# Two constants of a kernel's own scheduler: the transfer of loads planned a fifth longer, and six PSUM banks for attention in place of seven

## The chip, the cores and the metric

The kernel runs on one core of a Trainium2 chip. The metric is device time in microseconds (us), the median of several executions. One execution of each kernel was also profiled. Its span, from the first to the last instruction, is shorter than its own time (384.8 against 386.56 us for the kernel before). Comparisons between traces therefore use trace times alone.

Names: PE is TensorE (matmul), PEld its weight loads, DVE is VectorE, ACT is ScalarE, POOL is GpSimd, and SP is SyncE, which only issues DMAs here. A name such as SPq or POOLq is an engine's instruction queue. The argument rests on engines that keep to the order in which the program holds their instructions.

## The reference

A linear attention with a feature map comes first, then a feed-forward network (FFN) with a squared ReLU. There are 8 batches, 8 heads, 576 positions and a head dimension of 64.

```python
def phi(x):                                   # (b, h, s, 64) -> (b, h, s, 256)
    proj = einsum('bhsd,df->bhsf', x, w_phi)
    proj = proj - max(abs(proj), axis=-1, keepdims=True)
    return concatenate([exp(proj), exp(-proj)], axis=-1)
q_p, k_p = phi(q), phi(k)
kv, z = einsum('bhsf,bhsd->bhfd', k_p, v), sum(k_p, axis=2)
attn = einsum('bhsf,bhfd->bhsd', q_p, kv) / (einsum('bhsf,bhf->bhs', q_p, z)[..., None] + 1e-06)
x = attn.transpose(0, 2, 1, 3).reshape(4608, 512)
h = maximum(x @ w_in, 0.0)                    # w_in: 512 x 2048
out = (h * h) @ w_out                         # w_out: 2048 x 512
```

The FFN works on nine *chunks* of four tiles of 128 tokens. Each batch of attention makes four and a half such tiles. Below, a unit or a chunk starts when its first weight load does.

## The kernel before

The kernel does not write its instructions down in the order of its source. It first describes every piece of work as an `Op`, with an engine, a planned cost, a key for priority, the ops it depends on, and the buffers it takes. Then `Plan.order()` plays this list through in planned time, and the program is emitted in the order of the planned starts. The constants of the plan thus decide the order in which instructions stand in each engine's queue, and with it which buffer each op takes and how much filler PE gets. When the program runs, an instruction waits for its data and for the instruction ahead of it in its queue. The planned times exist no more.

```python
NATT, LEAD, DUE, SPAN = 7, 3, 26, 36
r_one = ring("one", 8, [P, 512], F32, ps)     # the eight PSUM banks
r_att = Ring(list(range(NATT)))               # so many of them may attention hold at once
...
def load(key, kb, rows, fn, deps=(), bufs=()):
    ...
    i = pl.op("pool", 780, key, fn, list(deps) + (full if n > 4096 else []), bufs, lat=0)
    issues.append(i)
    d = pl.op("dma", kb * 2.5, key, None, [i], bufs, lat=2600)   # planned transfer
    queue.append((n, d))
    return d
```

Four parts:

```python
# POOL issues the three loads (k, q, v) of a batch
nc.gpsimd.dma_start(out=buf.t[...], in_=rows[:, a:z, :])                 # L301

# SP transposes a finished attention tile into the FFN's input by a DMA
nc.sync.dma_start_transpose(out=xT.t[:, tt], in_=xo.t)                   # L652

# FFN in: one unit is four 512-column matmuls on PE; all units read the chunk's xT
nc.tensor.matmul(out=w.t[...], lhsT=win[...], rhs=xT.t[:, a:z, kc, :])   # L675
# then ACT applies ReLU (L680), and POOL squares, for chunks 0 to 6
nc.gpsimd.tensor_tensor(out=t.t, in0=r.t, in1=r.t, op=ALU.mult)          # L683
```

The DMA transposes of q and k (L352) are issued by SP as well. While PE has nothing to do at the start, the plan fills it with matmuls on a tile of ones (`warm`, L322), which are meant to keep its clock up.

Of the kernel before, what the change touches and what calls it, by code (L numbers as in the profile page):

```python
# [45 lines left out]
class Plan:  # L46
# [31 lines left out]
    def order(self):  # L78
        ready = {e: [] for e in sorted({o.eng for o in self.ops}, key=lambda e: (e != "x", e))}
        busy = {e: 0.0 for e in ready}  # L80
        rows = {e: None for e in ready}
        for o in self.ops:
            if o.n == 0:
                heapq.heappush(ready[o.eng], (o.key, o.seq, o))
        ev, now, done = [], 0.0, []

        def can(o):
            new = [x for x in o.bufs if x.slot is None]
            return all(x.can() and len(x.ring.free) >= sum(y.ring is x.ring for y in new)
                       for x in new)  # L90

        while True:
            for e, q in ready.items():
                if busy[e] > now:
                    continue
                skip = []
                while q:
                    it = heapq.heappop(q)
                    o = it[2]
                    if not can(o):  # L100
                        skip.append(it)
                        continue
                    for x in o.bufs:
                        if x.slot is None:
                            x.take()
                    o.start = now
                    end = now + o.cost
                    if o.rows is not None:
                        if rows[e] not in (None, o.rows):
                            end += self.SWITCH  # L110
                        rows[e] = o.rows
                    busy[e] = end
                    done.append(o)
                    same = [d for d in o.next if d.eng == e]
                    other = [d for d in o.next if d.eng != e]
                    for i, (t, what) in enumerate((
                            (end, ()), (end + 60, same), (end + o.lat, other),
                            (end + o.lat, None))):
                        heapq.heappush(ev, (t, 4 * o.seq + i, o, what))
                    break  # L120
                for it in skip:
                    heapq.heappush(q, it)
                if busy[e] <= now and e in self.idle and self.idle[e][2].start is None:
                    cost, fn, _ = self.idle[e]
                    o = Op()
                    o.eng, o.fn, o.start, o.cost, o.key = e, fn, now, cost(now), 1e9
                    busy[e] = now + o.cost
                    done.append(o)
                    heapq.heappush(ev, (busy[e], -len(done), o, ()))
            if not ev:  # L130
                break
            now = ev[0][0]
            while ev and ev[0][0] <= now:
                _, _, o, what = heapq.heappop(ev)
                if what is None:
                    for x in o.bufs:
                        x.left -= 1
                        if x.left == 0:
                            x.ring.free.append(x.slot)
                    continue  # L140
                for d in what:
                    d.n -= 1
                    if d.n == 0:
                        heapq.heappush(ready[d.eng], (d.key, d.seq, d))
        assert all(o.start is not None for o in self.ops)
        self.span = now
        return done
# [10 lines left out]
def kernel(  # L158
# [58 lines left out]
    r_h2 = ring("h2", 30, [P, TCH], BF16)  # L217
    r_ot = ring("ot", 2, [P, DM], F32)

    NATT, LEAD, DUE, SPAN = 7, 3, 26, 36  # L220

    r_one = ring("one", 8, [P, 512], F32, ps)
    r_att = Ring(list(range(NATT)))
# [2 lines left out]
    pl = Plan()  # L226
# [27 lines left out]
    def load(key, kb, rows, fn, deps=(), bufs=()):  # L254



        n = (queue[-1][0] if queue else 0) + rows
        full = [d for m, d in queue if m >= n - 4096][:1]
        i = pl.op("pool", 780, key, fn, list(deps) + (full if n > 4096 else []), bufs, lat=0)  # L260
        issues.append(i)
        d = pl.op("dma", kb * 2.5, key, None, [i], bufs, lat=2600)
        queue.append((n, d))
        return d

# [27 lines left out]
    def loads(b, dep=None):  # L293
        got = {}
        for i, (name, src, r) in enumerate((("k", k, r_xk), ("q", q, r_xq), ("v", v, r_xv))):
            buf = Buf(r)
            rows = src[b].rearrange("h s d -> (h s d)").rearrange(
                "(pr t c) -> t pr c", pr=NPR, t=P)

            def fn(a, z, buf=buf, rows=rows):  # L300
                nc.gpsimd.dma_start(  # L301
                    out=buf.t[:, a * NJ : z * NJ].rearrange("t (pr j) d -> t pr (j d)", j=NJ),
                    in_=rows[:, a:z, :],
                )
            key = FIRST + i if b == 0 else FIRST + (10, 13, 14)[i] if b == 1 else 32 * b - 120
            cut = (0, 2, 4) if b == 0 else (0, 4)
            got[name] = buf, [[load(key, 295 * (z - a), 128 * (z - a),
                                    lambda a=a, z=z, fn=fn: fn(a, z), [dep], [buf])]
                              for a, z in zip(cut, cut[1:])]
        return got  # L310
# [3 lines left out]
    win_v = moe_w_in.rearrange("(kc p) m -> p kc m", p=P)  # L314
    wout_v = moe_w_out.rearrange("(kc p) n -> p kc n", p=P)
    o_win = load(FIRST + 5, 4194, 512, lambda: nc.gpsimd.dma_start(out=win, in_=win_v))
    x1 = loads(1)
    o_wout = load(FIRST + 12, 4194, 2048, lambda: nc.gpsimd.dma_start(out=wout, in_=wout_v))

    def warm():  # L320
# [486 lines left out]
```

## Time and profile before

| | before |
|---|---|
| time | 386.79 us, median of 3 (385.71 to 387.05) |
| span of the profiled run | 384.8 us |
| PE busy | 368.5 us, 96% |
| filler matmuls | 274 |
| PE idle in the trace, gaps over 0.35 us, with the 1.1 us before its first matmul | 10.3 us |

The page of the kernel before, its head and three of its rows over 40 slices of 9.6 us each. A digit is tenths of a slice; PEclk is the clock that PE was granted.

```profile
span 384.8 us, 10484 instructions
...
PE 368.5 (96%) x4152; PEld 199.6 (52%) x4152; DVE 248.0 (64%) x554; ACT 244.1 (63%) x485; POOL 184.7 (48%) x310
...
PE   8899799999994999999999999999999999999994
...
PEclk9999989999996999999999999999999999999999
DMA  8999994349989442389559563964311232112123
```

PE is full in nearly every slice. The Trainium skill ("Trainium Kernel Development and Optimization", "Performance Expectations") warns that matmul busy time says little about the distance from the roofline, since matmuls are pipelined. It is used here only to find the holes, and a hole is where it is low. The table by windows (columns: window, its length, then busy us and instructions of PE, PEld, DVE, ACT, POOL, then granted clock, DMA share, GB/s; the DMA share adds up the times of packets, and these overlap, so it can pass 1) shows the two holes of the kernel before.

```profile
44.00:50.00 6.00, 3.94 (x50) 3.04 (x50) 5.72 (x11) 5.71 (x8) 5.15 (x5) 0.97 1.27 164
50.00:54.00 4.00, 4.00 (x76) 2.40 (x75) 3.83 (x11) 1.55 (x4) 1.25 (x2) 0.61 1.22 201
...
115.60:121.00 5.40, 0.57 (x5) 0.25 (x4) 3.23 (x7) 2.00 (x2) 0.00 (x0) 0.72 1.15 185
121.00:125.00 4.00, 4.00 (x14) 1.26 (x15) 0.42 (x1) 1.42 (x3) 0.37 (x2) 0.53 1.19 242
```

In the second hole PE does almost nothing for 5.4 us. It then works for 4 us at about half the clock. The chain of waits (start, length, what) names the cause.

```profile
109.27 1.26 SPq L352
110.53 0.04 issue
110.57 10.29 DMA qT_76<-xq_71
120.87 0.05 issue
120.91 0.28 PE one_157 L561
121.19 1.82 PE one_160 L704 x4
```

PE stood at the query projection of batch 3 (L561). Its input is a DMA transpose that took 10.29 us from issue to landing. The timeline of POOL shows what was under way then: the three loads of batch 4, issued from 108.72 us on.

```profile
108.72 0.81 POOL L301 DMA_DIRECT2D xk_68<-in_k_dram  x1 [0.36 <-issue]
109.52 0.75 POOL L301 DMA_DIRECT2D xq_70<-in_q_dram  x1
110.25 0.76 POOL L301 DMA_DIRECT2D xv_72<-in_v_dram  x1
```

### The profile page before, as it was taken

How to read it: one execution, taken by the hardware profiler on the slowest of the kernel's cores; microseconds unless marked ns; L12 is line 12 of the kernel's file. 1: busy time of each engine (PE TensorE's matmuls, PEld its weight loads, DVE VectorE, ACT ScalarE, POOL GpSimd, SP SyncE). 2: the span in 40 equal slices, each digit the busy share in tenths (PEclk: the TensorE clock that was granted, in tenths of full speed). 3: DMA queues.
4: the chain of work that ended last, by engine and by line, in shares of the span. 5: the costliest groups of instructions: out<-in, count | busy, mean ns of one | idle time of the engine just before them, and what ended most of it. 6: DMA issues, size and time to landing. Idle time of an engine off the chain costs nothing.

```text
span 384.8 us, 10484 instructions
## 1 busy us (share of the span) xinstructions
PE 368.5 (96%) x4152; PEld 199.6 (52%) x4152; DVE 248.0 (64%) x554; ACT 244.1 (63%) x485; POOL 184.7 (48%) x310
## 2 busy tenths in 40 slices
PE   8899799999994999999999999999999999999994
PEld 7788656544551455545544544455445454444442
DVE  2878977994693747894798468947893764233221
ACT  4795879568943796588649775887588653333300
POOL 8543846439940696297556656575445320000000
PEclk9999989999996999999999999999999999999999
DMA  8999994349989442389559563964311232112123
GB/s 124 211 208 204 168 188 87 75 75 210 101 126 206 89 57 48 72 139 151 111 89 200 80 115 63 200 121 95 70 27 31 49 64 53 44 27 55 28 61 75
DMA packets 70720, 40.39 MB, mean 105 GB/s; under 512 B 51088, under 2 KB 65552, under 8 KB 70672
## 3 DMA queue, kind: packets, MB, share of 16 engines
q1 hardware_dynamic: 55360, 21.38, 31.3%
q0 software_dynamic: 15312, 18.35, 29.1%
q8 instruction: 32, 0.52, 0.6%
q14 instruction: 16, 0.13, 0.1%
HBM read 36.77 MB, written 9.44 MB: 120 GB/s over the span
## 4 chain that ended last, share of the span: by engine, by line
PE 84%; DVE 7%; DMA 3%; ACT 2%; POOL 1%; SPq 1%; issue 1%; DVEq 0%
PE one_163 L704 6%; PE one_164 L675 5%; PE one_161 L704 5%; PE one_159 L704 5%; PE one_162 L675 4%; PE one_157 L675 4%; PE one_159 L675 4%; PE one_163 L675 4%; PE one_157 L704 4%; PE one_162 L704 4%; PE one_160 L675 3%; PE one_161 L675 3%; PE one_160 L704 3%; PE one_164 L322 3%; PE one_158 L675 3%; DMA qT_76<-xq_71 3%
## 5 line engine op out<-in xcount | busy, mean ns | idle before, releaser
L675 PEld LDWEIGHTS <-win 128*128 128x128 bf16 x704 | 59.2, 98 | 55.6 <-issue 5.2
L322 PE MATMUL one_164<-ones 128*128 128x128 bf16 x274 | 20.8, 233 | 1.1 <-DVE scrap L280 1.1
L574 POOL COPY mq_107<-m_104 64x4 f32<-64x4 f32 x52 | 9.6, 184 | 20.9 <-DVE m_104 L565 16.6
L322 PEld LDWEIGHTS <-ones 128*128 128x128 bf16 x274 | 17.6, 105 | 2.4 <-DVE scrap L280 1.1
L574 POOL COPY mq_108<-m_105 64x4 f32<-64x4 f32 x46 | 8.5, 184 | 11.7 <-DVE m_105 L565 10.3
L406 PEld LDWEIGHTS <-kT_74 64*128 64x128 bf16 x288 | 8.2, 94 | 8.8 <-issue 7.2
L574 POOL COPY mq_109<-m_106 64x4 f32<-64x4 f32 x46 | 8.5, 184 | 8.3 <-DVE m_106 L565 6.8
L680 ACT ACTIVATE hr_124<-one_160 128x512 bf16<-128x512 f32 x9 | 5.4, 596 | 8.6 <-PE one_160 L675 8.1
L683 POOL TENSOR_TENSOR h_141<-hr_123 128x512 bf16<-128x512 bf16 x4 | 4.2, 1039 | 11.6 <-ACT hr_123 L680 10.2
L675 PE MATMUL one_163<-xT_118,win 128*128 128x128 bf16 (+2 forms) x88 | 9.4, 253 | 0.3 <-ACT em_111 L581 0.2
L680 ACT ACTIVATE hr_123<-one_163 128x512 bf16<-128x512 f32 x9 | 5.3, 592 | 6.3 <-PE one_163 L675 5.7
L680 ACT ACTIVATE hr_122<-one_162 128x512 bf16<-128x512 f32 x9 | 5.4, 597 | 5.4 <-PE one_162 L675 5.3
L565 DVE TENSOR_REDUCE m_104<-one_162 128x4 f32<-128x512 f32 x6 | 4.1, 688 | 7.0 <-ACT hr_122 L680 4.9
L461 POOL TENSOR_TENSOR va_90<-xv_72,va_90 128x512 bf16<-128x512 bf16 (+1 forms) x5 | 6.2, 1244 | 5.0 <-ACT kph_80 L448 4.4
L561 PEld LDWEIGHTS <-qT_76 64*128 64x128 bf16 x144 | 4.4, 94 | 7.5 <-DMA qT_76<-xq_71 5.2
L683 POOL TENSOR_TENSOR h_143<-hr_122 128x512 bf16<-128x512 bf16 x4 | 4.2, 1044 | 8.3 <-ACT hr_122 L680 8.3
L532 PEld LDWEIGHTS <-wphi_61 64*128 64x128 bf16 x160 | 4.8, 94 | 6.2 <-issue 5.0
L435 ACT ACTIVATE kph_79<-ksh_88 128x1024 bf16<-128x1024 f32 x5 | 5.3, 1055 | 4.3 <-DVE ksh_88 L427 4.2
L610 PEld LDWEIGHTS <-qph_97 128*128 128x128 bf16 (+1 forms) x104 | 5.4, 101 | 4.7 <-issue 1.7
L680 ACT ACTIVATE hr_123<-one_161 128x512 bf16<-128x512 f32 x8 | 4.8, 604 | 4.3 <-PE one_161 L675 3.6
L565 DVE TENSOR_REDUCE m_105<-one_164 128x4 f32<-128x512 f32 (+1 forms) x7 | 4.5, 646 | 4.6 <-PE one_161 L561 4.1
L680 ACT ACTIVATE hr_123<-one_164 128x512 bf16<-128x512 f32 x9 | 5.4, 596 | 3.1 <-PE one_164 L675 3.1
(1001 smaller groups left out, 1365.2 us busy)
## 6 DMA issues: line engine op xcount, KB each, us to landing
out_dram<-ot_155 SPq DMA_DIRECT2D x36, 128.0 KB, 2.4
out_dram<-ot_156 SPq DMA_DIRECT2D x36, 128.0 KB, 2.4
xk_69<-in_k_dram POOLq DMA_DIRECT2D x4, 576.0 KB, 6.8
xq_71<-in_q_dram POOLq DMA_DIRECT2D x4, 576.0 KB, 9.9
xv_73<-in_v_dram POOLq DMA_DIRECT2D x4, 576.0 KB, 12.9
win<-in_moe_w_in_dram POOLq DMA_DIRECT2D x1, 2048.0 KB, 18.4
wout<-in_moe_w_out_dram POOLq DMA_DIRECT2D x1, 2048.0 KB, 31.0
xk_68<-in_k_dram POOLq DMA_DIRECT2D x3, 576.0 KB, 7.4
```

The lines of the kernel that those rows point to most:

```text
L322: nc.tensor.matmul(out=r_one.tiles[7][:, :P], lhsT=ones, rhs=ones, start=True, stop=True)
L406: nc.tensor.matmul(out=w[e].t[:, i * Fd : (i + 1) * Fd], lhsT=kT.t[r, u0 // 2 + i, :], rhs=wphi2[r, :], start=True, stop=True)
L435: nc.scalar.activation(out=t.t[:, :, : n // 2, :].rearrange("x e i f -> x e (i f)"), in_=ksh.t[:, :, : n // 2, :].rearrange("x e i f -> x ...
L461: v_.tensor_tensor(out=y.t[:, u0 : u0 + n, :D], in0=xv.t[:, u0 : u0 + n, :], in1=y.t[:, u0 : u0 + n, D].to_broadcast([P, n, D]), op=ALU.mult)
L532: nc.tensor.matmul(out=o[bk][:, r], lhsT=wphi2[x, :], rhs=qT.t[x, m : m + nj, :].rearrange("x m (hi p) -> x m hi p", hi=2), start=True, st ...
L565: d1 = [dve(kk, nj * 256, lambda w=w, m0=m0, nj=nj, bk=bk: nc.vector.tensor_reduce(out=m0.t[:, bk, : 2 * nj], in_=w[bk].t[:, : nj * 256].r ...
L574: nc.gpsimd.tensor_copy(out=mq.t[lo + jj * 64 : lo + jj * 64 + 64, :, :, hi], in_=m0.t[hi * 64 : hi * 64 + 64, :, : 2 * nj].rearrange("x b ...
L610: nc.tensor.matmul(out=nd(slice(0, D + 1))[:, z], lhsT=qg[s].t.rearrange("f pr hi p -> f (pr hi p)")[:, h * (hi_ - lo) : (h + 1) * (hi_ - ...
L675: nc.tensor.matmul(out=w.t[:, y * n : (y + 1) * n], lhsT=win[:, kc, mc * P : (mc + 1) * P], rhs=xT.t[:, a:z, kc, :], start=(kc == 0), stop ...
L680: o = act(key - 4, TCH, lambda: nc.scalar.activation(out=r.t, in_=w.t, func=ACT.Relu), [p_], [w, r])
L683: o = pool(key - 4, 1050, lambda: nc.gpsimd.tensor_tensor(out=t.t, in0=r.t, in1=r.t, op=ALU.mult), [o], [r, t])
L704: nc.tensor.matmul(out=w.t, lhsT=h2[c, mc, tt][0].t[:, h2[c, mc, tt][1] :][:, :P], rhs=wout[:, mc, :], start=(mc == 0), stop=(mc == KC2 - 1))
```

## The change

The intent: loads take longer on the chip than planned, and attention holds almost all PSUM banks. If the plan knew this, its order might fit the chip better.

```diff
-    NATT, LEAD, DUE, SPAN = 7, 3, 26, 36
+    NATT, LEAD, DUE, SPAN = 6, 3, 26, 36
...
-        d = pl.op("dma", kb * 2.5, key, None, [i], bufs, lat=2600)
+        d = pl.op("dma", kb * 3, key, None, [i], bufs, lat=2600)
```

(Two more lines of the diff give `o.lat` a local name and change nothing.) No work is added or removed except filler. The plan for the new constants starts the FFN later and fills PE with 316 matmuls on ones in place of 274. All else is order, and the choice of buffers that follows from it.

More of the change, by code (lines that the diff above doesn't have):

```diff
@@ L106, in order @@
                     o.start = now
-                    end = now + o.cost
+                    end, lat = now + o.cost, o.lat
                     if o.rows is not None:
@@ L116, in order @@
                     for i, (t, what) in enumerate((
-                            (end, ()), (end + 60, same), (end + o.lat, other),
-                            (end + o.lat, None))):
+                            (end, ()), (end + 60, same), (end + lat, other),
+                            (end + lat, None))):
                         heapq.heappush(ev, (t, 4 * o.seq + i, o, what))
```

## The prediction

> **What bounds it now.** TensorE (PE). The page gives PE 368.5 us busy of a 384.8 us span (96%), and 84% of the chain that ended last is PE. From 130 us the ten-microsecond windows show PE at 9.8 to 10.0 of 10. The rest lies in three places:
>
> 1. Start, 0 to 32.7 us: attention of batch 0 alone, with 274 filler matmuls on `ones`.
> 2. 44 to 54 us: PE busy 3.94 of 6 us, then the granted clock is 0.61.
> 3. 115.6 to 125 us: PE busy 0.57 of 5.4 us, then 4 us at clock 0.53. PE stands at batch 3's first query projection, whose transposes (qT_76, issued 110.57) landed only at 120.87, in 10.3 us where 2.4 us is usual. They share the DMA engines with batch 4's three loads (issued 108.7 to 110.3, landed by 123.0). The Trainium skill, "DMA: Bandwidth & Descriptors", section "Issuing engines are not separate DMA queues", says all DMAs run on the same 16 engines and interleave; the 10.3 us agree. The slow clock after the gap agrees with "TensorE: Matmul & The Clock Gate", Part 1 (half rate after idling): four 512-column matmuls then take 1.7 to 1.9 us, not 1.0.
>
> **What the change does.** Only filler is added: the two constants reorder static queues. The compared orders show:
>
> - 42 more filler matmuls (316) before the first FFN unit. At 56 ns each that is 2.35 us, inside batch 0's start, where seven PSUM banks become six. Part replaces a 2 us wait for GpSimd. Net cost: 1 to 2 us.
> - At 45 us, four FFN output units move ahead of the second half of chunk 0's inputs. They need w_out, which lands at 47.7 us, so the stall at 44 to 54 us stays about equal, with another cause.
> - Batch 3's first query projection moves about 9 us of PE work later, behind three units of FFN chunk 2. This removes the stall on qT_76. But chunk 2's first unit needs batch 2's third activation transpose (xT_120). In the kernel before it was issued at 111.97, 3.3 us after the loads began, and landed at 123.30, hidden behind the qT stall. GpSimd's queue reaches batch 4's loads about 4 us later and this transpose is issued still about 3 us after them, so it should land about 14.5 us after the loads begin. PE has only about 11 us of work before chunk 2. I expect a stall of 5 to 8 us there, with about 1.7 us of slow clock after it.
> - From batch 5 on the PE order is nearly the same. No gain there.
>
> **Predicted.** Start +1 to +2 us, 44 to 54 us about 0, the stage at 110 to 130 us about 0 to +2 us: **389 us**, range 383 to 394. Faster by over 2%: 0.05; within 2%: 0.86; slower by over 2%: 0.09.
>
> **What would show it.** First FFN unit at 33.5 to 35 us in place of 32.65. No wait of PE on qT_76, but a PE gap of over 4 us before the first chunk-2 unit at about 115 to 128 us, ended by an xT_120 transpose that took about 10 us.
>
> **What would make it wrong.** If that transpose is issued before batch 4's loads (it then lands in 2.4 us), most of the 7 to 8 us hole vanishes and the time is near 382. If filler at the start counts fully and w_out holds PE up longer, it is near 393.

## The result

The changed kernel takes **400.84 us** (median of 4, 398.75 to 401.86), against 386.92 us (385.71 to 387.86) for the kernel before. The ratio is 1.0355, with a 95% interval of 1.0304 to 1.0405. It is slower by 14 us, where 2 us were predicted. PE's idle gaps over 0.35 us sum to 22.6 us in the trace, against 10.3 before, counted in the same way. Ratios here and below are the mean time of one kernel's runs over that of the other's in the same rounds, so they are not quite the ratio of the medians quoted. The kernels of one set of experiments ran on the same chip, and the median of before was 385 to 387 us in all of them. Every 95% interval quoted below lies wholly on one side of 1, though some reach across 2%.

The page after, the same rows. In the profile of the changed kernel, names stand without buffer numbers, and 45 of 4194 matmul records are missing.

```profile
span 399.1 us, 10529 instructions
...
PE 367.3 (92%) x4149; PEld 200.7 (50%) x4194; DVE 248.6 (62%) x554; ACT 244.2 (61%) x485; POOL 184.9 (46%) x310
...
PE   8989799978893999859999999999999999999995
...
PEclk9999999999998899969999999999999999999999
DMA  8999974459769315992248944695411132211123
```

PE's busy time is about the same. The span grew by idle time, and PE's row has two deep dents (3 and 5) where before had one. The windows around them:

```profile
121.70:128.70 7.00, 0.03 (x1) 0.02 (x1) 2.83 (x7) 1.06 (x1) 0.00 (x0) 0.82 1.26 190
128.70:133.00 4.30, 4.29 (x11) 1.51 (x12) 0.00 (x0) 2.14 (x3) 1.03 (x1) 0.50 0.85 199
...
168.00:174.30 6.30, 0.00 (x0) 0.00 (x0) 3.91 (x8) 0.03 (x1) 0.00 (x0) 0.71 1.28 169
174.30:178.00 3.70, 3.69 (x11) 1.40 (x12) 0.00 (x0) 1.73 (x3) 1.02 (x1) 0.58 0.86 224
```

The first dent is the predicted one, before chunk 2's first FFN unit. The second, before chunk 3's, has no counterpart before and nobody predicted it. The chain of waits of the changed kernel gives both the same cause:

```profile
117.00 11.57 DMA xT<-xo
128.57 0.14 issue
128.71 4.87 PE one L675 x12
...
163.41 10.85 DMA xT<-xo
174.26 0.05 issue
174.31 4.28 PE one L675 x12
```

Each time PE stands at the chunk's first unit (L675), whose activation transpose takes 11 us to land. In each case the clock records show half of full clock for 6.8 us, from within the gap on. Each time POOL had issued a batch's three loads 2.2 to 3.3 us earlier. POOL's timeline after, at the second dent, shows where these loads stand in the queue: right behind the last small copy of batch 3's attention, with no square of chunk 3 ahead of them.

```profile
160.43 0.86 POOL L574 COPY mq<-m 64x4 f32<-64x4 f32 x4 [1.72 <-DVE m L565]
161.23 0.81 POOL L301 DMA_DIRECT2D xk<-in_k_dram  x1
162.02 0.76 POOL L301 DMA_DIRECT2D xq<-in_q_dram  x1
162.75 0.77 POOL L301 DMA_DIRECT2D xv<-in_v_dram  x1
```

The same loads in POOL's timeline *before*:

```profile
160.81 1.04 POOL L683 TENSOR_TENSOR h_143<-hr_122 128x512 bf16<-128x512 bf16 x1 [6.99 <-ACT hr_122 L680]
161.81 1.04 POOL L683 TENSOR_TENSOR h_144<-hr_123 128x512 bf16<-128x512 bf16 x1
163.10 1.04 POOL L683 TENSOR_TENSOR h_145<-hr_124 128x512 bf16<-128x512 bf16 x1 [0.25 <-ACT hr_124 L680]
164.08 0.81 POOL L301 DMA_DIRECT2D xk_69<-in_k_dram  x1
164.87 0.76 POOL L301 DMA_DIRECT2D xq_71<-in_q_dram  x1
165.60 0.77 POOL L301 DMA_DIRECT2D xv_73<-in_v_dram  x1
```

This is the difference that matters at that place, as a run below shows. In the kernel before, three squares of chunk 3 stand ahead of batch 5's loads. A square cannot run before its matmuls, and those cannot run before the chunk's transpose has landed. So the loads could not start before the transpose was done (issued at 153.80 us, landed at 156.21). No semaphore said so. The order of POOL's queue did. In the changed plan the loads moved ahead of those squares, and the accidental protection was gone. A late transpose alone costs nothing: in the kernel before, one issued at 165.09 us, 1.0 us behind these loads, took 8.91 us as well, but its chunk started only at 193.8 us.

### The profile page after: what moved, and what is told of

Same layout as the page of the kernel before. It is cut to its first block, busy times and chain, and to the rows that moved or that the text cites. A ratio compares the mean times of both kernels' runs of the same rounds, so it can differ in the third digit from the quotient of the medians.

```text
span 399.1 us, 10529 instructions
## 1 busy us (share of the span) xinstructions
PE 367.3 (92%) x4149; PEld 200.7 (50%) x4194; DVE 248.6 (62%) x554; ACT 244.2 (61%) x485; POOL 184.9 (46%) x310
## 4 chain that ended last, share of the span: by engine, by line
PE 75%; DMA 16%; DVE 3%; issue 2%; ACT 2%; POOL 1%; POOLq 0%; DVEq 0%; ACTq 0%
PE one L675 30%; PE one L704 28%; DMA wout<-in_moe_w_out_dram 8%; DMA xT<-xo 6%; PE one L610 5%; PE one L494 4%; DMA xv<-in_v_dram 2%; PE one L532 2%; PE one L561 2%; PE one L406 2%; ACT kph L435 1%; DVE mk L417 1%; POOL va L461 1%; DVE ksh L427 1%; ACT hr L680 1%
## 5 line engine op out<-in xcount | busy, mean ns | idle before, releaser
L683 POOL TENSOR_TENSOR h<-hr 128x512 bf16<-128x512 bf16 x112 | 115.3, 1040 | 106.4 <-ACT hr L680 103.6
L675 PE MATMUL one<-xT,win 128*128 128x512 bf16 (+2 forms) x704 | 149.2, 347 | 14.4 <-DMA xT<-xo 13.3
L704 PE MATMUL one<-wout,h 128*128 128x512 bf16 x531 | 138.0, 380 | 5.5 <-issue 2.1
L680 ACT ACTIVATE hr<-one 128x512 bf16<-128x512 f32 x144 | 85.2, 600 | 80.3 <-PE one L675 77.8
L675 PEld LDWEIGHTS <-win 128*128 128x128 bf16 x704 | 59.1, 99 | 68.4 <-issue 14.9
L542 ACT ACTIVATE qph<-one 128x512 bf16<-128x512 f32 (+1 forms) x160 | 78.8, 566 | 16.7 <-PE one L532 15.2
L704 PEld LDWEIGHTS <-h 128*128 128x128 bf16 x576 | 50.5, 98 | 56.7 <-issue 3.2
L435 ACT ACTIVATE kph<-ksh 128x1024 bf16<-128x1024 f32 (+1 forms) x70 | 65.0, 966 | 22.0 <-DVE ksh L427 21.8
L565 DVE TENSOR_REDUCE m<-one 128x4 f32<-128x512 f32 (+1 forms) x80 | 48.1, 631 | 43.7 <-PE one L561 31.7
L417 DVE TENSOR_REDUCE mk<-one 128x4 f32<-128x512 f32 (+1 forms) x80 | 49.7, 627 | 4.3 <-PE one L406 4.2
L427 DVE TENSOR_TENSOR ksh<-one,mk 128x512 f32<-128x512 f32 (+1 forms) x70 | 44.7, 638 | 3.9
```

The source lines that it names most:

```text
L417: nc.vector.tensor_reduce(out=mk.t[:, e, ms], in_=wv(e), axis=AX.X, op=ALU.max, apply_absolute_value=True)
L427: nc.vector.tensor_tensor(out=ksh.t[:, e, : n // 2, :], in0=wv(e), in1=mk.t[:, e, ms].to_broadcast([P, n // 2, Fd]), op=ALU.subtract)
L435: nc.scalar.activation(out=t.t[:, :, : n // 2, :].rearrange("x e i f -> x e (i f)"), in_=ksh.t[:, :, : n // 2, :].rearrange("x e i f -> x ...
L542: nc.scalar.activation(out=t.t.rearrange("f pr hi p -> f (pr hi p)")[:, : nj * 512].rearrange("f (r b c) -> f b r c", r=2, b=2)[:, bk], in ...
L565: d1 = [dve(kk, nj * 256, lambda w=w, m0=m0, nj=nj, bk=bk: nc.vector.tensor_reduce(out=m0.t[:, bk, : 2 * nj], in_=w[bk].t[:, : nj * 256].r ...
L675: nc.tensor.matmul(out=w.t[:, y * n : (y + 1) * n], lhsT=win[:, kc, mc * P : (mc + 1) * P], rhs=xT.t[:, a:z, kc, :], start=(kc == 0), stop ...
```

## The experiments

The theory, called the **load collision**: a DMA transpose issued behind a batch's loads lands late, up to some 9 us, because they share the DMA engines (for the sharing the prediction cites its source; what the runs show is the lateness). PE then stands still when the next FFN chunk starts with it. Rivals: **six banks** starve attention all along, or the additional **filler** at the start costs the time.

Most experiments move instructions *after* planning, so that nothing else changes. For the loads of batch `b`:

```python
done = pl.order()
def put(b, c, i):               # batch b's loads to just behind the square of chunk c, unit i
    at = h2[c, i, 0][2]
    for o in issued[b]:
        done.remove(o)
    k = done.index(at) + 1
    done[k:k] = issued[b]
```

A comparison of the built programs showed the same order on PE, DVE, ACT and SP, and a moved group on POOL alone. The traces of the runs with moves agree. All kernels but one gave correct results; the exception is marked.

### Only the longer loads

```diff
-        d = pl.op("dma", kb * 2.5, key, None, [i], bufs, lat=2600)
+        d = pl.op("dma", kb * 3, key, None, [i], bufs, lat=2600)
```

> Only the longer planned loads, seven banks. Theory (load collision: GpSimd's queue reaches a batch's three loads before the first square of the next FFN chunk, so the activation transpose that the chunk's first PE unit waits for is issued amid the loads and lands 10 us late): here batch 4's loads stand ahead of chunk 2's squares, as in both kernels, but batch 5's stand behind chunk 3's first square. So one PE gap of 4 to 8 us before chunk 2 and none over 1 us before chunk 3; about 391 to 394 us. Rival (six banks starve attention, and that is the loss): about 387 us, as before, for seven banks are kept.

Measured: 396.23 us, ratio 1.0254 (1.0190 to 1.0319). There is one gap of 7.67 us before chunk 2 and none before chunk 3, as expected. The time is 2 us over the range. Chunk 1 already starts at 85.5 us against 81.3 us before, after several waits of PE for DVE of under 1 us each, and from 83.1 us the clock was at half for 6.8 us, which it was not there before. So part of this loss lies ahead of any collision named here. The rival of six banks fails for this run: with all seven, the kernel is 2.5% slower than before.

### Only six banks

```diff
-    NATT, LEAD, DUE, SPAN = 7, 3, 26, 36
+    NATT, LEAD, DUE, SPAN = 6, 3, 26, 36
```

> Only six banks, loads planned as before. Here the loads of batch 4 and of batch 5 both stand ahead of the first square of chunk 2 and chunk 3. Collision theory: two PE gaps, 4 to 8 us each, before chunks 2 and 3; 397 to 403 us. Rival (banks): near 400 us as well, but with the time lost in many short waits of PE, not in two gaps.

Measured: 404.18 us, ratio 1.0469 (1.0387 to 1.0551), 1 us over the range. The waits of PE (engine, line, what it waited for: total us, times, longest) are led by two gaps, 6.35 us before chunk 2 and 4.78 us before chunk 3:

```profile
PE one L675 <- DMA xT<-xo: 11.1, 2, 6.3
PE one L704 <- issue: 2.2, 14, 0.2
PE one L704 <- DMA wout<-in_moe_w_out_dram: 2.0, 1, 2.0
```

The gaps are as the theory said, but they are not the whole loss. Of the 16.9 us between the spans (401.7 against 384.8), 8.0 us stand already when chunk 1 starts (89.3 against 81.3 us), and the clock was at half for 6.8 us from 87.3 us, which it was not there before. What six banks cost in this early stretch was not isolated.

The two constants do not add: 2.5% and 4.7% alone, 3.6% together. So no cost can be assigned to either by itself. Each draws another order.

### The changed kernel, batch 5's loads put back behind chunk 3's third square

```diff
+    put(5, 3, 2)
```

> The changed kernel with batch 5's three load instructions moved in GpSimd's queue behind the third square of chunk 3, as in the kernel before; the order of PE, VectorE, ScalarE and SyncE is untouched, filler and six banks stay. Collision theory: the 6.3 us PE gap before chunk 3 and the 1.8 us of slow clock after it go; 391 to 393.5 us (0.976 to 0.982 of the changed kernel). Rivals (six banks; filler at the start): no more than 1 us gained, 400 us.

Measured: 391.76 us, ratio 1.0145 (1.0083 to 1.0207). That is 9 us below the changed kernel (8.1 us by the ratios), by the move of three instructions in one queue, and it lies inside the range that was predicted for the change. The gap before chunk 3 is gone; the 6.36 us before chunk 2 remain. Six banks and all filler are still there, so neither can be what those 9 us were.

### The kernel before, batch 4's loads behind chunk 2's first square

```diff
+    put(4, 2, 0)
```

> The kernel before with batch 4's loads moved behind the first square of chunk 2; nothing else moves. Collision theory: query transposes of batch 3 and the activation transpose land in about 2.5 to 4 us, the hole at 115 to 125 us closes to under 1 us; 379 to 381 us. If the hole has another cause, or is only put off to batch 4's own transposes: 385 to 388 us.

Measured: 383.07 us, ratio 0.9926 (0.9864 to 0.9987). The hole at 115 us closed: chunk 2 starts at 118.0 us in place of 124.5. So that hole, too, came from the loads. But of these 6.5 us only 4.2 were left when chunk 3 started (154.6 in place of 158.8 us), and the time misses the range. POOL's timeline shows where:

```profile
134.71 2.10 POOL L389 COPY va<-xv 128x2304 bf16<-128x2304 bf16 x1 [3.17 <-DMA xv<-in_v_dram]
136.78 2.04 POOL L683 TENSOR_TENSOR h<-hr 128x512 bf16<-128x512 bf16 x2
```

The loads now land later. POOL reached its copy of batch 4's V before V was there and stood 3.17 us, with the squares of chunk 2 behind it.

### The same, and the copy of V moved back too

```diff
+    put(issued[4], 2, 0)
+    put(copies[4], 2, 14)        # copies[b]: POOL's copy of batch b's V
```

> The kernel before with batch 4's loads behind chunk 2's first square, and GpSimd's copy of batch 4's V, which stood 3.2 us at the head of its queue waiting for that load, moved behind chunk 2's square 14. If that copy caused the 2 us given back at 132 to 139 us: PE waits there vanish; 2 us below the run without it, 381 us, 0.98 to 0.988 of before. If the loads' own later landing caused it: no gain, 0.993.

Measured: 380.11 us (379.57 to 381.35, 6 runs), ratio 0.9836 (0.9794 to 0.9877). From chunk 2's start to chunk 3's this trace takes 35.2 us, against 36.6 with the copy in its old place and 34.3 in the kernel before. By these traces the copy made 1.3 of the 2.3 us given back; where the rest went was not traced. The times differ by more (3 us), but the two runs belong to different sets. This is the fastest kernel: 1.6% faster than before and 5% faster than the change.

### The kernel before, with the suspect put in: batch 5's loads ahead of chunk 3

```diff
+    put(5, 2, 15)
```

> The kernel before with batch 5's three loads moved forward in GpSimd's queue, behind the last square of chunk 2 and so ahead of chunk 3's first; nothing else moves. Collision theory: the loads begin at about 151 us, the activation transpose for chunk 3 (issued at 153.8) lands near 164 us in place of 156, and a PE gap of 4 to 7 us opens before chunk 3: 391 to 395 us, 1.015 to 1.025 of before. Rivals (six banks, filler): no change, for both are as before.

Measured: 393.94 us, ratio 1.0183 (1.0135 to 1.0230). The loads begin at 151.21 us. The transpose for chunk 3 is issued at 153.81 us, as in the kernel before (153.80), but its line in the chain of waits now reads

```profile
153.81 9.44 DMA xT<-xo
```

in place of 2.4 us, and PE waits 4.11 us before chunk 3. Seven banks and 274 filler matmuls do not protect from it. The same transpose at the same time, with or without loads ahead of it, is the cleanest single proof of the theory.

### The changed kernel without the additional filler

```diff
+            if o.fn is warm:
+                warms += 1
+                if 137 < warms:
+                    continue
```

> The changed kernel with only its first 137 filler pairs, as many as before has; the 21 later pairs are not issued. Rival (filler at the start is the cost): 6 us or more gained, under 395 us. Collision theory: at most 2 us gained (2.35 us of filler, part of which covers waits), with both gaps still there; 398.5 to 401 us.

Measured: 396.96 us, ratio 1.0255 (1.0202 to 1.0307). The gain is 4 us, twice what was allowed for the filler. The trace shows that it is not filler's own time. The first FFN unit comes 2.1 us earlier (34.1 us against 36.1), but PE then waits longer for w_out (2.30 us against 1.44), its clock falls to half for 3.4 us from 49.2 us, which it did not in the changed kernel, and chunk 1 starts at 84.7 us against 84.0. Nothing is left of it there. What changed are the two gaps, 4.23 and 5.20 us against 6.98 and 6.32. The first transpose for chunk 2 was issued 1.2 us behind the loads in place of 3.3 and landed 11.7 us after they began in place of 14.84. So small shifts upstream change the size of a gap. Why the second gap also shrank, with its transpose 2.2 us behind the loads in both kernels, was not settled.

### Both batches' loads late in the changed kernel

```diff
+    put(5, 3, 2)
+    put(4, 2, 0)
```

> The changed kernel with batch 4's loads behind chunk 2's first square and batch 5's behind chunk 3's third. Collision theory: both gaps go; from the 391.8 us of batch 5's alone another 6.4 us of gap and 1.7 us of slow clock, less the 2 us that came back in the kernel before (GpSimd's copy of V waits for the later load): 385 to 387 us. What is then left over before is the start and the planning of the first 100 us.

Measured: 383.57 us, ratio 0.9920 (0.9874 to 0.9966). Both gaps are gone, and with them more than the whole loss. It beats the range because the 2 us did not come back: here the copy of V stands later in the queue by itself and waited under 0.1 us. With the collisions removed, the kernel with six banks, longer planned loads and 42 more filler matmuls is no slower than before. It stays 3.5 us above the best order drawn from the kernel before.

### The same, without the additional filler

The edit is the two moves above and the filler count above together.

> Both batches' loads late in the changed kernel (383.6 us) and 21 filler pairs less. With the gaps gone, what does filler cost? In the changed kernel the 2 us that it gave at the first FFN unit were used up by chunk 1 (84.7 against 84.0 us), in a longer wait for w_out; its 4 us came from transposes that were issued sooner after the loads, so from shorter gaps. Then 0 to 1 us gained here: 382.5 to 384 us. If filler costs its own time: 381 to 381.5 us or less.

Measured: 382.14 us, ratio 0.9893 (0.9855 to 0.9931), just under the range. This interval and that of the run with the filler (0.9874 to 0.9966) overlap for the most part, and the profiled spans are 381.1 and 381.4 us. The ratios differ by 0.0027, or 1 us, which is less than either interval is wide. So filler's own cost is about 1 us at the best estimate, and not told apart from none.

### A third of the bytes (a wrong result)

```diff
+    for o in issued[5][1:]:      # batch 5's q and v are not loaded
+        done.remove(o)
```

> A wrong result on purpose: the changed kernel without batch 5's loads of Q and V (it reads batch 3's in their buffers), so that only K's load, a third of the bytes, begins ahead of the transposes for chunk 3; no instruction is moved. If the bytes ahead of a transpose on the shared DMA engines set its landing: the transpose that landed after 10.8 us lands after 4 to 6 us, the 6.3 us gap before chunk 3 shrinks to under 1.5 us, and the time falls to 392 to 395 us. If it is the load instructions or their place alone, and not their bytes: gap and time stay, 399 to 401 us.

Measured: 392.62 us, ratio 1.0140 (1.0076 to 1.0203), and the result is wrong, as meant. The load of K still stands ahead of the transpose, which was issued 1.2 us behind it:

```profile
162.67 5.89 DMA xT<-xo
```

It landed after 5.89 us in place of 10.85, and PE's wait before chunk 3 fell below 0.5 us. The distance does not explain this: in the run with less filler, a transpose issued 1.2 us after the first of three loads took 10.52 us. So the amount of loading ahead of the transpose sets its landing, not its place alone. Bytes, packets and load instructions fell together here, and no run separates them, nor tells what within the DMA makes the transpose wait.

## Why the prediction was wrong

The time was 400.84 us against 389 and a range of 383 to 394. The runs split the loss. From the ratios, times 386.9 us:

| term | from which runs | us |
|---|---|---|
| collision before chunk 3, new | 1.0355 − 1.0145 | +8.1 |
| collision before chunk 2 | 1.0145 − 0.9920 | +8.7 |
| the hole that before had there | 0.9836 − 1 | −6.3 |
| what remains: the early part, by the traces | 0.9920 − 0.9836 | +3.2 |
| sum | | +13.7 |

The sum closes by construction, and each ratio carries an interval of some 2 us each way, so a difference of two about 3 us. The spans of the profiled runs split the 14.3 us between the traces alike: 8.5, 9.2, −6.8 and 3.4 us.

- **"From batch 5 on the PE order is nearly the same. No gain there."** This is the step that failed. As a statement on PE's order it holds. But it closed the search between chunk 2 and batch 5: no one asked where batch 5's *loads* stood in POOL's queue in relation to chunk 3's squares. They had moved ahead of them, and this cost 8.1 us. The mechanism had been read correctly one chunk earlier and was not looked for at its next occurrence. The compared orders of POOL would have shown their new place before any run. With these loads alone put back, the kernel took 391.76 us, inside the predicted range.
- **The stall before chunk 2** was right in mechanism and size: predicted 5 to 8 us, measured 6.98; ended by a late xT transpose, which landed 14.84 us after the loads began (14.5 predicted) and took 11.57 us (about 10 predicted). PE had no wait on the query transposes. The net against before was put at 0 to +2 us and is +2.4.
- **The start** was put at +1 to +2 us. The first FFN unit came at 36.1 us, later than the predicted 33.5 to 35, and about 3.2 us remain at the end. In the traces of the two kernels compared for it (both loads late in the changed kernel; the fastest), 2.8 of 3.5 us are there at the first FFN unit: 35.6 against 32.8 us. Filler is about 1 us of it at the best estimate, by the last run without it. Which waits make up the rest stays open. The trace shows 1.44 us for w_out, 1.86 us for ACT and 1.42 us for DVE there, but no run took each away alone.
- **44 to 54 us "about equal, with another cause"**: w_out was the new wait, as predicted. The slow clock that before had there (0.61 in 50 to 54 us) was 1.00 after, so the stage was no worse.
- **The named risk** ("If filler at the start counts fully and w_out holds PE up longer, it is near 393") looked at the start. The real risk was a second collision, and it was missing from the list.

## What to carry to other kernels

In a program like this one, what protects a latency-critical transfer from bulk loads may be nothing but an instruction's place in another engine's queue. If a re-planned order changes, check for every bulk load which short transfers are due within its next 10 to 15 us (the late transposes here landed 12 to 15 us after the loads began), on every engine's queue and at every repetition, not only where a trace showed the first case. And bind such loads explicitly behind the first consumer of the short transfer. The kernel does so for batch 3 alone (`pl.after` with chunk 1's first square). Here moved loads made the kernel before 1.6% faster, together with the moved copy of V, and the changed one 4% faster. When loads are moved later, look for the in-order instruction that waits for them.

## What the Trainium skill lacked or had wrong

- "DMA: Bandwidth & Descriptors", "Issuing engines are not separate DMA queues", says that all DMAs share 16 engines and interleave. It gives no time for a short transfer that meets a long one. Here a transpose that lands in 2.4 us alone took 9.4 to 11.6 us when issued 2 to 3 us behind three loads (together 3 × 8 × 576 × 64 × 4 bytes, 3.5 MB read), and 5.9 us behind one of the three. At the second dent it landed (174.26 us) after the loads of K and Q (168.25 and 172.88) and before that of V (176.15), as if it had waited for most of what was ahead of it.
- The same page, "Rules for kernel authors", says "A transpose next to ordinary DMAs needs nothing". For correctness no run contradicts it; for time, one such meeting cost 8.1 us of 400.
- "TensorE: Matmul & The Clock Gate", "Why this matters for your kernels", warns of PE-idle gaps of about 3 us or more. The two gaps of over 6 us agree: half clock for 6.8 us by the trace's clock records in each case, from 4.5 us into the first gap (126.2 us) to 4.3 us after its end. That row gives no size for several short gaps close together. In the kernel before, three gaps of 0.67, 0.86 and 1.04 us within 5 us were followed by a clock of 0.61 in 50 to 54 us, and with the same order of PE and the same three gaps it stayed at 1.00 there in the fastest kernel. So such a group of gaps was followed by the slow clock in one execution and not in another.
- None of the pages named here states that the order of one engine's queue can keep its loads off another engine's transfers without a semaphore. Three squares on GpSimd kept GpSimd's loads off SyncE's transposes here, and were worth 8.1 us.
